# One table of a state-space backward pass is built in the stage that uses it instead of two stages earlier

## The chip, the cores and the metric

The kernel runs on one core of one Trainium2 chip. The metric is device time in microseconds, the median of several executions. One execution was also taken by the hardware profiler; its page and its trace are what the text reads. TensorE is PE in the profile (PEld is its load of weights), VectorE is DVE, ScalarE is ACT, GpSimd is POOL, SyncE is SP. SP, ACT and POOL issue DMAs.

## What is computed

The reference is a block with two branches over x (2048 rows of 512 columns), and the kernel returns its output and all gradients for an incoming gradient:

```python
xn = layernorm(x)
s  = ssm(xn)                  # y = causal convolution of xn with K along the 2048 rows, + xn * Dskip
g  = silu(silu(xn @ w1) @ w2) # w1: 512 x 1792, w2: 1792 x 512
out = x + s * g
# K[d, l] = Re sum_n C[d,n] * exp(dt[d] * A[d,n] * l) * dt[d] * B[d,n],  n = 0..127, A, B, C complex
```

The gradients of A, B and C need, for each channel d and state n, sums over l of dK[d, l] times the power exp(dt A l). The powers are the tables of this text. A position l is split into a coarse and a fine part, l = 128 h + 8 w (with some special positions), so that each power is a product of a coarse table X (41 entries a channel) and a fine table Y (16 entries a channel: exponents 0, 8, ..., 120). CY is Y multiplied by C and dt B; it is used for K itself.

## The kernel before

The kernel is six stages written one behind the other; inside each stage the order of instructions on every engine is the order in which the Python calls them (the scheduling is manual), and generators are advanced step by step to lay the work of several parts beside one another.

**Stage 1** (0 to about 180 us in the trace) runs the feed-forward branch and computes base powers of the tables for all channels (`power_phases`, L427), which go to DRAM as `XYd`: 28 entries, of which 0 to 16 are bases for X, 17 to 19 the low bases of Y (exponents 8, 16, 24), 20 to 23 its high bases (0, 32, 64, 96) and 24 to 27 the high bases of CY.

**Stage 2**, here called the table stage (about 180 to 300 us), goes through four blocks b of 128 channels. For each block, `open_tables` (L751) loads X's bases, `ld_tab` (L743) loads the eleven entries of Y and CY as XYc, `copy_tables` (L781) spreads them with ScalarE copies into tiles Y and CY (L786), and `chunk_tables` (L795) multiplies out X (`prod`, L816 to L823), CY and Y (`quads`, L802 to L813) on the DVE. A call of `quads` is six DVE instructions: one product of 3072 elements a partition (L806), two of 1536 (L810), and two sums of 1536 (L811, L813). `chunk_K` (L848) multiplies CY by X on TensorE (ps_k, L860), and ScalarE puts the result into Kout; after block 3, `store_K` (L872) writes K to DRAM as Kud and `load_K` (L885) brings it back in another layout as K_b. `gen_xt` (L921) transposes X on TensorE in eleven groups (L932), ScalarE evicts them (L934), and SP stores them to DRAM as XTd; `gen_yt` (L941) does the same with Y, in two calls of two groups a block (L950, L951), to YTd. XT and YT share four buffers of one tag. Beside these, the loop of `stage_2` runs forward transforms of xn and of DS on TensorE (ps_f, L998, evicted by L999), a radix step on the DVE (`radix`, L92 to L98), and transposes of w2 (L973 to L977).

The order in the loop over j (L1054 to L1076): Y's product of block b (`next(k.gt[b])`, L1062) is called at j = 0 of block b for b = 0 and 1, the one of block 2 at L1078, that of block 3 at L1093. X's bases of block b + 2 are loaded at j = 10 (L1074), on the SP queue behind the XTd stores of block b.

**Stage 3 and stage 4** (about 300 to 440 us) transform K_b (ps_f, L1164), multiply spectra on the DVE (`cplx_mul`, L101) and transform back. The last XT and YT groups of block 3 are evicted between these transforms.

**Stage 5** has two halves. The first ends at about 480 us. The second, here called the slab stage (480 to 575 us), lays three things beside one another on TensorE: `conv` (L1680; 16 matmuls of 512 columns, ps_v), the gradient of w2 (`Dw2.run`, L1589; two halves of 8 matmuls of 512 columns, ps_w), and the **slabs** (`Slabs`, L1717). A slab is a quarter of a block: 16 slabs, three steps each (`steps`, L1809):

- step A: `P2(i, 0)`, 16 matmuls of 256 columns (ps_V, L1769) evicted by ScalarE to Vb (L1771); then `Gb(i + 1)` on the DVE (two instructions, L1757).
- step B: `P2(i, 1)`, the same for the other half; then `load(i + 3)`, which issues the slab's XT (XTl, on SP and POOL) and its YT (YTl, on POOL, L1747).
- step C: `D3(i)` on the DVE (three instructions, L1780 and L1783), Vb times YT; then `P3(i - 1)`, eight matmuls of 512 columns (ps_S, L1798) of the slab before.

The loop over ft from 4 to 13 (L1693) places them: a conv while there is one (ft 4 to 9), one step, half a w2 product, two steps, the other half, two steps. PSUM has two buffers for ps_v and ps_V together (tag pd) and three for ps_w and the transposes (tag ps).

**Stage 6** (575 us to the end) is the backward pass of the feed-forward branch, led by `dh` (L1857).

The few lines that set the order of the slab stage:

```python
for ft in range(4, FT):
    t0 = 2 * (ft - 2)
    if t0 < T:
        conv(t0)
    some(1)
    for _ in w2.run(ft):
        some(2)
    some(2)
```

Of the kernel before, what the change touches and what calls it, by code (L numbers as in the profile page):

```python
# [14 lines left out]
P = 128  # L15
# [120 lines left out]
def kernel(ctx, tc, A_u, A_A_re, A_A_im, A_B_re, A_B_im, A_C_re, A_C_im, A_log_dt, A_Dskip, B_x, B_w1, B_w2, grad_out,  # L136
# [28 lines left out]
    k.XTd = dr.tile([NB, 64 * NR, 2, P], BF16, name="XTd"); k.YTd = dr.tile([16, P, 2, 4, P], BF16, name="YTd")  # L165
# [556 lines left out]
def tables_open(k, fs):  # L722

    lo = k.left
    k.mm = lo.open("mm")
    sa = lo.open("sa")
    k.tabs, k.gt, k.gc = {}, {}, {}
    k.slot = [(sa, sa), None]
    XY = fs.tile([P, 11, 2, 64, 2], BF16, name="XYc", tag="aT")

    def more():
        k.nc.gpsimd.dma_start(XY[:].rearrange("p i c q e -> p i (c q e)"), k.XYd[:, 17:NT, 0])
# [4 lines left out]
    k.gt[0] = chunk_tables(k, 0)  # L737
    k.nt0 = 0
    k.ko = lo.open("ko"); k.xc = lo.open("xc")
    k.Kout = k.ko.tile([P, NH, P], BF16, name="Kout")  # L740


def ld_tab(k, b):  # L743

    XY = k.xc.tile([P, 11, 2, 64, 2], BF16, name="XYc", tag="XYc")
    k.nc.sync.dma_start(XY[:].rearrange("p i c q e -> p i (c q e)"), k.XYd[:, 17:NT, b])
    k.gc[b] = copy_tables(k, b, XY)
    k.gt[b] = chunk_tables(k, b)
# [13 lines left out]
def open_y(k, b):  # L762

    slot, cys = k.slot[b % 2]
    k.tabs[b]["Y"] = slot.tile([P, 2, 64, 16, 2], BF16, name="Y", tag="Y")
    k.tabs[b]["CY"] = cys.tile([P, 2, 64, 16, 2], BF16, name="CY", tag="CY")
# [13 lines left out]

def copy_tables(k, b, XY):  # L781

    Y, CY = k.tabs[b]["Y"], k.tabs[b]["CY"]
# [11 lines left out]
def chunk_tables(k, b):  # L795
# [6 lines left out]
    def quads(x, op0, op1):  # L802
        fl = lambda m: m.rearrange("p c q (a b) e -> p (c q) a b e", a=4)
        m1, m2 = mt("m1", 12), mt("m2", 12)
        qd = x[:].rearrange("p c q (a b) e -> p c q a b e", a=4)
        TT(out=fl(m1), in0=qd.rearrange("p c q a b e -> p (c q) a b e")[:, :, :, 0:1].to_broadcast([P, 128, 4, 3, 2]),  # L806
           in1=cq(t["Y"], slice(1, 4)).unsqueeze(2).to_broadcast([P, 128, 4, 3, 2]), op=ALU.mult)
        q4 = lambda m, c: m[:, c].rearrange("p q (a b) e -> p q a b e", a=4)
        for c in range(2):
            TT(out=q4(m2, c), in0=qd[:, c, :, :, 0:1].to_broadcast([P, 64, 4, 3, 2]), in1=t["Y"][:, 1 - c, :, 1:4].unsqueeze(2).to_broadcast([P, 64, 4, 3, 2]), op=ALU.mult)  # L810
        TT(out=qd[:, 0, :, :, 1:4], in0=q4(m1, 0), in1=q4(m1, 1), op=op0)  # L811
        i, j = (0, 1) if op1 == ALU.add else (1, 0)
        TT(out=qd[:, 1, :, :, 1:4], in0=q4(m2, i), in1=q4(m2, j), op=op1)  # L813
# [18 lines left out]
    if b == 0:  # L832
        quads(t["CY"], ALU.add, ALU.subtract)
        yield
# [6 lines left out]
    if b:  # L841
        quads(t["CY"], ALU.add, ALU.subtract)
        yield
    quads(t["Y"], ALU.subtract, ALU.add)
    yield

# [74 lines left out]
def gen_xt(k, xs, b):  # L921

    nc = k.nc
    X = k.tabs[b]["X"][:].rearrange("p h c e q -> p h c (e q)")
    for n in range(11):
        ks = range(4 * n, min(4 * n + 4, 41))
        if n % 2 == 0:
            XT = xs.tile([P, 8, 2, P], BF16, name="XT", tag="XT", bufs=4)
        pt = k.ps.tile([P, 4, 2, P], BF16, name="pt_xt", tag="ps")
        for j, kk in enumerate(ks):  # L930
            for c in range(2):
                nc.tensor.transpose(out=pt[:, j, c], in_=X[:, kk, c], identity=k.ident[:])  # L932
# [5 lines left out]
        yield  # L938


def gen_yt(k, xs, i0):  # L941
    nc = k.nc
    YT = xs.tile([P, 2, 2, 4, P], BF16, name="YT", tag="XT", bufs=4)
    for i in (i0, i0 + 1):
        b, u, s, q0 = slab(i)
        Y = k.tabs[b]["Y"]
        pt = k.ps.tile([P, 2, 4, P], BF16, name="pt_yt", tag="ps")
        for c in range(2):
            for b4 in range(4):
                nc.tensor.transpose(out=pt[:, c, b4, :], in_=Y[:, c, q0 + 4 * b4:q0 + 4 * b4 + 4].rearrange("p w l e -> p (w l e)"), identity=k.ident[:])  # L950
        nc.scalar.copy(out=YT[:, i - i0], in_=pt[:])  # L951
        if i > i0:
            k.put(k.YTd[i0:i0 + 2].rearrange("i p c b n -> p i (c b n)"), YT[:].rearrange("p i c b n -> p i (c b n)"))
        yield
# [48 lines left out]
def stage_2(k):  # L1003
# [35 lines left out]
    for b in range(NB):  # L1039
# [3 lines left out]
        gy = [gen_yt(k, k.xs, i) for i in (4 * b, 4 * b + 2)]  # L1043
        sl = [gx] * 11 + [g for g in gy for _ in range(2)]
# [4 lines left out]
        if b == 2:  # L1049
            sl, gy2 = sl[:11], sl[11:]  # L1050
# [3 lines left out]
        for j in range(15):  # L1054
# [6 lines left out]
            if j == 0 and b < 2:  # L1061
                next(k.gt[b])  # L1062
# [15 lines left out]
    next(k.gt[2])  # L1078
    for g in gy2:
        next(g)  # L1080
# [12 lines left out]
    next(k.gt[3])  # L1093
    sl = iter(sl)
    for n in range(8):
        next(next(sl))
# [18 lines left out]
    return gk, sl, held  # L1115
# [151 lines left out]
def stage_3(k, gk, sl, held):  # L1267
# [3 lines left out]
    for n, _ in enumerate(gk, 1):  # L1271
# [4 lines left out]
        for g in (next(sl, None) for _ in range(n >= 4)):  # L1276
            if g is not None:
                next(g)
# [325 lines left out]
def stage_5(k):  # L1604
# [60 lines left out]
    S.load(0, nc.gpsimd)  # L1665
    for j in (1, 2):
        nc.gpsimd.memset(S.flat(j), 0.0)
# [49 lines left out]
class Slabs:  # L1717
# [3 lines left out]
    def __init__(self, k, sw):  # L1721
        self.k, self.sw = k, sw
        self.XT, self.YT, self.G, self.V, self.T, self.psS, self.S_sb = {}, {}, {}, {}, {}, {}, {}
# [14 lines left out]
    def load(self, i, q=None):  # L1738
        k, nc = self.k, self.k.nc
        dma = (q or nc.sync).dma_start  # L1740
        YT = self.YT[i] = self.sw.tile([P, 2, 4, P], BF16, name="YTl", tag="YT", bufs=4)
# [5 lines left out]
        nc.gpsimd.dma_start(YT[:], k.YTd[i])  # L1747
# [85 lines left out]
class Bwd:  # L1833
# [23 lines left out]
    def dh(self, n):  # L1857
# [5 lines left out]
        sd = self.fw.tile([P, 2, 512], BF16, name="sd", tag="sd")  # L1863
# [37 lines left out]
    def dx(self, tc_, dhT):  # L1901
# [3 lines left out]
        for t in range(4 * tc_, 4 * tc_ + 4):  # L1905
# [6 lines left out]
            m12 = fw.tile([P, 2], F32, name="m12", tag="m12"); c12 = fw.tile([P, 2], F32, name="c12", tag="c12")  # L1912
# [9 lines left out]
    def rest(self):  # L1922
# [8 lines left out]
        O1 = fw.tile([P, D], BF16, name="O1", tag="O1")  # L1931
# [7 lines left out]
def stage_6(k):  # L1939
# [5 lines left out]
    k.fx = ro.open("fx", 2)  # L1945
# [64 lines left out]
    ro.close("fp4", "ww", "fx", "fw", "wt", "tip", "tf2", "tfp")  # L2010
# [31 lines left out]
```

## Time and profile before

| | us |
|---|---|
| median of 3 executions | 753.71 |
| lowest, highest of them | 752.43, 753.82 |
| the profiled execution | 754.35 |
| its span (first to last instruction) | 752.2 |
| TensorE busy | 665.2 (88%) |
| DVE busy | 619.8 (82%) |
| ScalarE busy | 444.4 (59%) |
| POOL busy | 124.4 (17%) |

The span lies inside the profiled execution's time; 2.15 us of that execution are around it. Times inside the text count from the span's start. "Idle before, releaser" in the profile's rows says how long an engine stood before an instruction and what ended that. A row of a timeline gives the start, the time that it covers, the engine, the line, what is written and read, and how many instructions are merged in it. Instructions of one engine overlap a little at their ends, so that a sequence takes less than the sum of its rows.

### The profile page before, as it was taken

What the parts mean: (1) busy time and instruction counts of PE and PEld (TensorE: products, weight loads), DVE (VectorE), ACT (ScalarE), POOL (GpSimd) and SP (SyncE); (2) the same over time, 40 slices, a digit from 0 to 9 for tenths busy, and PEclk for the clock granted to TensorE, in tenths of its full rate; (3) what the DMA queues carried; (4) which work ended last, traced back from release to release, by engine and by line L of the source; (5) the groups of instructions that cost most, each with busy time, mean ns of one, the idle gap of its engine ahead of it and who ended that gap; (6) DMA issues with size and microseconds to landing.
All of it is one profiled execution on the core that took longest, in us unless ns stands there. A gap on an engine that the chain in (4) does not pass through costs nothing. (4 is left out here: it accounts for less than half of the span.)

```text
span 752.2 us, 13787 instructions
## 1 busy us (share of the span) xinstructions
PE 665.2 (88%) x5356; PEld 347.0 (46%) x5356; DVE 619.8 (82%) x965; ACT 444.4 (59%) x541; POOL 124.4 (17%) x192
## 2 busy tenths in 40 slices
PE   4768978798978777999999899989999999889998
PEld 2434444353646566454444344434444554444444
DVE  6899999998999798699999999654685579988810
ACT  4789888986769857375435322244566765764211
POOL 2334071021002003000012111311131000111210
PEclk9999998999989997999999999999999999999999
DMA  9647766899898969899667889798895987788591
GB/s 270 235 160 254 239 212 240 273 315 362 266 318 280 289 189 215 302 375 380 247 248 250 298 324 339 227 331 303 279 298 170 283 230 225 234 251 280 186 344 52
DMA packets 153155, 198.86 MB, mean 264 GB/s; under 512 B 29405, under 2 KB 114788, under 8 KB 147170
## 3 DMA queue, kind: packets, MB, share of 16 engines
q1 hardware_dynamic: 133314, 129.48, 54.6%
q0 software_dynamic: 11840, 54.07, 20.0%
q10 hardware_dynamic: 7936, 14.43, 5.9%
q8 instruction: 42, 0.69, 0.4%
q14 instruction: 23, 0.19, 0.1%
HBM read 112.72 MB, written 83.38 MB: 261 GB/s over the span
## 5 line engine op out<-in xcount | busy, mean ns | idle before, releaser
L607 PE MATMUL ps_h<-XNT,W 128*128 128x512 bf16 x224 | 61.1, 423 | 13.8 <-ACT hs L610 13.8
L1188 PEld LDWEIGHTS <-TIs 128*128 128x128 bf16 x384 | 37.3, 98 | 50.4 <-issue 4.4
L580 PE MATMUL ps_o<-W,aT 128*128 128x512 bf16 x224 | 54.3, 391 | 1.8 <-DVE ak L76 1.8
L1869 PE MATMUL ps_da<-DOT,W2T 128*128 128x512 bf16 x224 | 52.9, 379 | 1.5 <-ACT DOT L1849 1.1
L1908 PE MATMUL ps_dx<-W1T,dhT 128*128 128x512 bf16 x224 | 52.9, 379 | 0.0
L1870 DVE TENSOR_TENSOR dhT<-ps_da,sd 128x1024 bf16<-128x1024 f32 x28 | 34.1, 1221 | 22.0 <-ACT sd L132 16.3
L1594 PE MATMUL ps_w<-DO_all,AW 128*128 128x512 bf16 x224 | 52.0, 380 | 0.0
L1992 PE MATMUL ps_w<-dhc,xn 128*128 128x448 bf16 x256 | 49.3, 352 | 1.0 <-DMA dhc<-dhd 1.0
L1780 DVE TENSOR_TENSOR T<-Vb,YTl 128x2048 bf16<-128x2048 bf16 x16 | 19.6, 1223 | 35.9 <-ACT Vb L1771 35.6
L1164 PEld LDWEIGHTS <-TFs 128*128 128x128 bf16 x312 | 30.2, 98 | 37.4 <-issue 2.8
L934 ACT COPY XT<-pt_xt 128x1024 bf16<-128x1024 bf16 (+1 forms) x44 | 41.3, 1004 | 4.0 <-DMA XTd<-XT 3.0
L1771 ACT CAST Vb<-ps_V 128x1024 bf16<-128x1024 f32 x32 | 31.7, 1013 | 17.9 <-PE ps_V L1769 12.0
L607 PEld LDWEIGHTS <-W 128*128 128x128 bf16 x224 | 22.7, 105 | 39.4 <-issue 22.8
L1164 PE MATMUL ps_f<-K_b,TFs 128*128 128x512 bf16 x168 | 38.9, 379 | 1.7 <-DMA K_b<-Kud 1.2
L1917 ACT ACTIVATE dxn<-dxn,c,rstd 128x512 f32<-128x512 f32 x16 | 13.0, 814 | 45.0 <-DVE c L1916 45.0
L580 PEld LDWEIGHTS <-aT 128*128 128x128 bf16 x224 | 22.8, 102 | 31.2 <-issue 7.4
L1992 PEld LDWEIGHTS <-xn 128*128 128x128 bf16 x256 | 25.0, 98 | 24.9 <-DMA dhc<-dhd 1.5
L998 PE MATMUL ps_f<-xn,TFs 128*128 128x512 bf16 x128 | 33.1, 414 | 2.4 <-DMA TFs<-TFd 2.4
L1893 ACT COPY dhk<-pt_dh 128x1024 bf16<-128x1024 bf16 x28 | 28.0, 1001 | 10.2 <-PE pt_dh L1891 10.2
L1869 PEld LDWEIGHTS <-W2T 128*128 128x128 bf16 x224 | 21.6, 98 | 26.8 <-issue 2.2
L1164 PE MATMUL ps_f<-DS,TFs 128*128 128x512 bf16 x144 | 33.0, 379 | 0.7 <-ACT S_s L1442 0.7
L1594 PEld LDWEIGHTS <-AW 128*128 128x128 bf16 x224 | 20.2, 98 | 26.7 <-issue 4.7
(345 smaller groups left out, 1570.6 us busy)
## 6 DMA issues: line engine op xcount, KB each, us to landing
TIs<-TId SPq DMA_DIRECT2D x24, 512.0 KB, 6.5
XTd<-XT SPq DMA_DIRECT2D x20, 512.0 KB, 4.5
XTl<-XTd SPq DMA_DIRECT2D x15, 512.0 KB, 8.1
hTd<-hs SPq DMA_DIRECT2D x28, 256.0 KB, 3.5
akd<-ak SPq DMA_DIRECT2D x28, 256.0 KB, 3.6
UXl<-UXd POOLq DMA_DIRECT2D x7, 1024.0 KB, 7.9
dhd<-dhk SPq DMA_DIRECT2D x28, 256.0 KB, 5.3
XYd<-XYg SPq DMA_DIRECT2D x25, 256.0 KB, 4.5
```

The source lines that it names most:

```text
L580: nc.tensor.matmul(out=pso[:], lhsT=aT[:, ft, tt * P:(tt + 1) * P], rhs=W2[:, ft, :], start=(ft == 0), stop=(ft == FT - 1))
L607: nc.tensor.matmul(out=ps[:, j], lhsT=W1[:, dk, ft * P:(ft + 1) * P], rhs=XNT[:, dk], start=(dk == 0), stop=(dk == DK - 1))
L934: nc.scalar.copy(out=XT[:, j0:j0 + len(ks)], in_=pt[:, 0:len(ks)])
L998: nc.tensor.matmul(out=ps[:, c, :], lhsT=TFs[:, t1 + 4 * j, c, :], rhs=src[:, t1 + 4 * j, :], start=(j == 0), stop=(j == 3))
L1164: nc.tensor.matmul(out=ps[:, c, :], lhsT=tab(j), rhs=at(t1 + 4 * j), start=(n == 0), stop=(n == 4 * len(terms) - 1))
L1188: nc.tensor.matmul(out=ps[:, j, :], lhsT=TIs[:, j, 2 * kt + c, :], rhs=B[kt][:, c, (t0 + j) % 4, :], start=(kt == 0 and c == 0), stop=(kt ...
L1594: nc.tensor.matmul(out=ps[:], lhsT=A[:, t, :], rhs=k.DO[:, t, :], start=(t == 0), stop=(t == T - 1))
L1771: nc.scalar.copy(out=self.V[i][:, g2], in_=ps[:].rearrange("p b c n -> p c b n"))
L1869: nc.tensor.matmul(out=ps[:, j], lhsT=self.W2T[:, ft // 2, dk, j * P:(j + 1) * P], rhs=self.DOT[tc_][:, dk], start=(dk == 0), stop=(dk == ...
L1870: nc.vector.tensor_tensor(out=self.dhT[:, f0:f0 + 2, :], in0=ps[:], in1=sd[:], op=ALU.mult)
L1908: nc.tensor.matmul(out=psx[:], lhsT=dhT[:, ft, t % 4 * P:(t % 4 + 1) * P], rhs=self.W1T[:, ft, :], start=(ft == 0), stop=(ft == FT - 1))
L1992: nc.tensor.matmul(out=ps[:], lhsT=k.xn[:, t, dk * P:(dk + 1) * P], rhs=ch[i][:, t, :], start=(t == 0), stop=(t == T - 1))
```

## The change

Y is no longer built, transposed or stored in the table stage. The tile Y, `gen_yt`, the DRAM tensor YTd and the loads YTl go. What is left of Y in the table stage is its three low bases (tile Yb), which CY's product needs; XYc has seven entries instead of eleven. XT has six buffers instead of four, and all eleven groups of block 3 are transposed in the table stage.

In the slab stage, `load_y` loads the seven bases of a block from XYd on POOL (XYl and XYo); `Yq(i)` spreads a slab's high bases with two ScalarE copies of 128 elements a partition (and, once a block, the low bases with one of 768) and multiplies the slab's Y out on the DVE in six instructions of 384 elements; `Yt(i)` transposes it on TensorE in eight 128x128 blocks, and ScalarE evicts them to YT. `Yq(i + 1)` is called in step B of slab i, `Yt(i + 1)` in step C behind `P3(i - 1)`. In stage 6, sd, m12, c12 and O1 move to a pool of their own, opened when the slabs' memory is given back.

```diff
 def copy_tables(k, b, XY):
-    def cp(x, o, i, n):
-        k.nc.scalar.copy(out=cq(x, o), in_=XY[:, i:i + n].rearrange("p i c q e -> p (c q) i e"))
-    cp(Y, slice(1, 4), 0, 3)
     yield
-    cp(Y, slice(0, 16, 4), 3, 4)
+    low_copy(k, k.tabs[b]["Yb"], XY[:, 0:3])
     yield
-    cp(CY, slice(0, 16, 4), 7, 4)
+    k.nc.scalar.copy(out=cq(k.tabs[b]["CY"], slice(0, 16, 4)), in_=XY[:, 3:7].rearrange("p i c q e -> p (c q) i e"))
     yield
...
+def cplx_quads(k, x, low, m1, m2, op0, op1):
...
+    else:
+        for c in range(2):
+            TT(out=q4(m1, c), in0=ba(c), in1=lw(c), op=ALU.mult)
+    for c in range(2):
+        TT(out=q4(m2, c), in0=ba(c), in1=lw(1 - c), op=ALU.mult)
+    TT(out=qd[:, 0, :, :, 1:4], in0=q4(m1, 0), in1=q4(m1, 1), op=op0)
+    i, j = (0, 1) if op1 == ALU.add else (1, 0)
+    TT(out=qd[:, 1, :, :, 1:4], in0=q4(m2, i), in1=q4(m2, j), op=op1)
...
 def chunk_tables(k, b, XY):
...
-    quads(t["Y"], ALU.subtract, ALU.add)
-    yield
...
 def gen_xt(k, xs, b):
...
-            XT = xs.tile([P, 8, 2, P], BF16, name="XT", tag="XT", bufs=4)
+            XT = xs.tile([P, 8, 2, P], BF16, name="XT", tag="XT", bufs=6)
...
-def gen_yt(k, xs, i0):
...
 class Slabs:
     def load(self, i, q=None):
...
-        nc.gpsimd.dma_start(YT[:], k.YTd[i])
+
+    def load_y(self, b):
+        k = self.k
+        ld = {}
+        for nm, o, n, bufs in (("XYl", 20, 4, 2), ("XYo", 17, 3, 1)):
+            t = ld[nm] = self.sw.tile([P, n, 2, 64, 2], BF16, name=nm, tag=nm, bufs=bufs)
+            k.nc.gpsimd.dma_start(t[:].rearrange("p i c q e -> p i (c q e)"), k.XYd[:, o:o + n, b])
+        self.XY[b] = ld["XYl"], ld["XYo"]
+
+    def Yq(self, i):
+
+        k, nc = self.k, self.k.nc
+        b, u, s, q0 = slab(i)
+        XY, low = self.XY[b]
+        if i % 4 == 0:
+            Yb = self.Yb = self.sw.tile([P, 2, 64, 3, 2], BF16, name="Yb", tag="Yb")
+            low_copy(k, Yb, low[:])
+        Y = self.Y[i] = self.sw.tile([P, 2, 16, 16, 2], BF16, name="Ys", tag="Ys", bufs=1)
+        for c in range(2):
+            nc.scalar.copy(out=Y[:, c, :, 0:16:4], in_=XY[:, :, c, q0:q0 + 16].rearrange("p a q e -> p q a e"))
+        m1, m2 = (self.sw.tile([P, 2, 16, 12, 2], BF16, name=f"Ym{j}", tag=f"Ym{j}") for j in range(2))
+        cplx_quads(k, Y[:], self.Yb[:, :, q0:q0 + 16], m1[:], m2[:], ALU.subtract, ALU.add)
+
+    def Yt(self, i):
+        k, nc = self.k, self.k.nc
+        Y = self.Y.pop(i)
+        pt = k.ps.tile([P, 2, 4, P], BF16, name="pt_yt", tag="ps")
+        for c in range(2):
+            for b4 in range(4):
+                nc.tensor.transpose(out=pt[:, c, b4, :], in_=Y[:, c, 4 * b4:4 * b4 + 4].rearrange("p w l e -> p (w l e)"), identity=k.ident[:])
+        YT = self.YT[i] = self.sw.tile([P, 2, 4, P], BF16, name="YT", tag="YT", bufs=2)
+        nc.scalar.copy(out=YT[:], in_=pt[:])
...
             self.P2(i, 0)
             if i + 1 < 16:
                 self.Gb(i + 1)
+            if i == 0:
+                self.Yq(0)
             yield
             self.P2(i, 1)
             self.XT.pop(i), self.G.pop(i)
             if i + 3 < 16:
                 self.load(i + 3)
+            if i % 4 == 1 and i < 12:
+                self.load_y(i // 4 + 1)
+            if i == 0:
+                self.Yt(0)
+            if i + 1 < 16:
+                self.Yq(i + 1)
             yield
             self.D3(i)
             if i:
                 self.P3(i - 1)
+            if i + 1 < 16:
+                self.Yt(i + 1)
...
-        sd = self.fw.tile([P, 2, 512], BF16, name="sd", tag="sd")
+        sd = k.fw2.tile([P, 2, 512], BF16, name="sd", tag="sd")
```

More of the change, by code (lines that the diff above doesn't have):

```diff
@@ L164 @@
     k.Snd = dr.tile([2, 2, D, N], F32, name="Snd")
-    k.XTd = dr.tile([NB, 64 * NR, 2, P], BF16, name="XTd"); k.YTd = dr.tile([16, P, 2, 4, P], BF16, name="YTd")
+    k.XTd = dr.tile([NB, 64 * NR, 2, P], BF16, name="XTd")
     k.dhd = dr.tile([P, T, F], BF16, name="dhd")
@@ L740, in tables_open, with ld_xy @@
     k.Kout = k.ko.tile([P, NH, P], BF16, name="Kout")
+def ld_xy(k, XY, b, q):
+    for o, i, n in ((0, 17, 3), (3, 24, 4)):
+        q.dma_start(XY[:, o:o + n].rearrange("p i c q e -> p i (c q e)"), k.XYd[:, i:i + n, b])
 def ld_tab(k, b):
-    XY = k.xc.tile([P, 11, 2, 64, 2], BF16, name="XYc", tag="XYc")
-    k.nc.sync.dma_start(XY[:].rearrange("p i c q e -> p i (c q e)"), k.XYd[:, 17:NT, b])
+    XY = k.xc.tile([P, 7, 2, 64, 2], BF16, name="XYc", tag="XYc")
+    ld_xy(k, XY, b, k.nc.sync)
     k.gc[b] = copy_tables(k, b, XY)
-    k.gt[b] = chunk_tables(k, b)
+    k.gt[b] = chunk_tables(k, b, XY)
 def open_tables(k, b, q, fn=None):
@@ L801, in chunk_tables, with quads @@
     mt = lambda nm, n: k.mm.tile([P, 4096], BF16, name=nm, tag="cm_t" + nm[1])[:, 0:256 * n].rearrange("p (c q n e) -> p c q n e", c=2, q=64, e=2)
[L802 to L813, printed above, removed]
+    def quads():
+        cplx_quads(k, t["CY"][:], t["Yb"][:], mt("m1", 12), mt("m2", 12), ALU.add, ALU.subtract)
     Xf = X[:].rearrange("p h c e q -> p h c (e q)")
@@ L937, in gen_xt @@
             k.put(k.XTd[b, P * k0:P * k1].rearrange("(k p) c n -> p k c n", p=P), XT[:, 0:k1 - k0])
-        yield
-def gen_yt(k, xs, i0):
[L942 to L953, printed above, removed]
         yield
@@ L1042, in stage_2 @@
         gx = gen_xt(k, k.xs, b)
-        gy = [gen_yt(k, k.xs, i) for i in (4 * b, 4 * b + 2)]
-        sl = [gx] * 11 + [g for g in gy for _ in range(2)]
+        sl = [gx] * 11
         if b == 3:
@@ L1092, in stage_2 @@
     radix(3)
[L1093 to L1096, printed above, removed]
+    for g in sl:
+        next(g)
     XD = st["D"]["A"]
@@ L1114, in stage_2 @@
     k.dskb = dskip_out(k)
-    return gk, sl, held
+    return gk, held
 def rad_inv(k, pool, tag, PX):
@@ L1264, in gen_kt, with stage_3 @@
         yield
-def stage_3(k, gk, sl, held):
+def stage_3(k, gk, held):
     nc = k.nc
```

52 lines of the change are left out of this document (26 added, 26 removed).

## Prediction

> **What bounds the kernel now.** I read the page's busy shares first, then the busy time by stretches, then the DVE's and TensorE's rows in order of time, and last the waits of single lines. A difference of 0.2% (1.5 us) is about what a measurement of this kernel can tell from no change.
>
> Busy time by stretches (us; busy time and count of each engine, granted clock, DMA share, GB/s):
>
> ```profile
> 240.00:260.00 20.00, 15.91 (x338) 12.38 (x334) 15.87 (x28) 18.47 (x22) 1.82 (x3) 0.91 0.98 298
> 380.00:420.00 40.00, 39.30 (x184) 17.73 (x182) 39.22 (x38) 15.95 (x18) 7.18 (x14) 1.00 0.82 285
> 500.00:520.00 20.00, 17.94 (x180) 8.04 (x179) 9.60 (x14) 8.53 (x10) 3.17 (x6) 1.00 0.96 337
> 540.00:560.00 20.00, 19.33 (x237) 8.84 (x234) 15.78 (x22) 12.52 (x15) 5.83 (x11) 1.00 0.87 290
> ```
>
> There are three regimes. In the table stage (first row) ScalarE, DVE and the DMA engines are all near full and hand the limit to one another. From 314 to 480 us the DVE has no gap to speak of, so whatever the table stage gains arrives whole at 480. In the slab stage (last two rows; 480.6 to 575.7) TensorE is the bound, its instructions stand in a fixed order, and the DVE is half idle at first and four fifths busy later. The change takes work out of the first regime and puts it into the third, and the order of instructions says that it does: no Y is multiplied or transposed before the slab stage.
>
> **Table stage: what goes.** The rows of the DVE in order of time:
>
> ```profile
> 250.69 1.22 DVE L98 TENSOR_TENSOR XU<-r_t 128x2048 bf16<-128x2048 bf16 x1
> 255.97 1.09 DVE L819 TENSOR_TENSOR m<-X 128x1792 bf16<-128x1792 bf16 x1 [4.06 <-DMA X<-XYd]
> ...
> 271.57 0.95 DVE L813 TENSOR_TENSOR CY<-m 128x1536 bf16<-128x1536 bf16 x1
> 272.44 1.75 DVE L806 TENSOR_TENSOR m<-Y 128x3072 bf16<-128x3072 bf16 x1
> ```
>
> Y's products are six instructions a block, 1.75 + 2x0.95 + 0.96 + 0.95 = 5.5 us, in queue 5.3. Four blocks give 22 us of DVE time, but only blocks 0 and 1 (193.5 and 225.2 us) stand ahead of block 3's CY, which ends at 272.4 and starts the way to the kernel's K: TensorE's ps_k, Kout, Kud, K_b, and at 302.4 the transform that keeps the DVE full from 314. Blocks 2 and 3 come after it. So 10.6 us are on the path, not 22. With these gone the DVE waits earlier for X: it already waits 4.06 us for block 3's X (above), which is loaded on SP behind the last XTd store, which follows ScalarE's 44 XT evictions. ScalarE has one gap (1.85 us) between 223.6 and 249.3. Ahead of that it loses block 0's four YT evictions (0.92 each in queue), the strided copy of Y (1.22) and, because XT gets six buffers of its own and no slot that YT held, the 5.2 us that it waited for an XTd store from 216.6 to 221.8: 10 us. SP's queue and the DMA engines give some of that back, so I take block 3's X 8 us earlier (its issue at 242.5 against 250.9); CY moves by 8, not 10.6. Two YTd stores of 512 KB stand on SP and in the DMA engines (share 0.97) just ahead of K_b's loads, which take 14 us to land; without them I take 2 us more. TensorE must be ready then: without pt_yt (279.3 to 284.2) it does two classes, eleven XT groups instead of eight at ScalarE's 0.92 each, and ps_dsk, and comes out at 291 to 292, about where K_b lands. Sum **-10 us**; bounds -5 (SP and the DMA engines keep X where it was but for the shorter queue) and -14 (10.6 and the whole of the DMA time of the two stores, 1 MB at 290 GB/s). The smaller XYc load is inside this; ScalarE's remaining low copy (0.88) was there before. Stage 3 loses four YT groups (0.45 us of TensorE and 1.02 of ScalarE each) that lie beside a full DVE: nothing.
>
> **Slab stage: what comes.** For slab i+1, in program order: step B of slab i issues P2(i,1) with its Vb eviction, then Yq(i+1) (two ScalarE copies of 128 elements, six DVE products of 384); step C issues D3(i) on the DVE, then P3(i-1) and the eight transposes of Yt(i+1) on TensorE. The copies are queued on ScalarE behind the Vb that waits for P2(i,1), the products behind the copies, the transposes behind P3(i-1), with all of TensorE's later work behind the transposes. A slab ahead is thus a third of a slab ahead. Prices by form:
>
> ```profile
> L806 DVE TENSOR_TENSOR m<-Y 128x3072 bf16<-128x3072 bf16 x4 | 7.0, 1750 | 0.0
> L95 DVE TENSOR_TENSOR r_t<-XU 128x512 bf16<-128x512 bf16 x5 | 2.1, 418 | 0.0
> L819 DVE TENSOR_TENSOR m<-X 128x256 bf16<-128x256 bf16 x4 | 1.1, 282 | 0.0
> ```
>
> 384 elements lie between the last two: 0.35 us each, and in a queue these rows start 0.07 to 0.08 earlier than their lengths say, so 0.27; six are 1.63 us. A 128-element copy is not in the trace: ScalarE's 128x256 XT piece takes 0.41 to 0.48, a 128x4 activation 0.20; I take 0.3, in queue 0.2, bounds 0.15 and 0.4.
>
> Now the order of time on TensorE, with what waits where:
>
> ```profile
> 491.15 0.62 PE L1769 MATMUL ps_V<-XTl,Gbd 128*32 128x256 bf16 x16
> 491.70 1.90 PE L1594 MATMUL ps_w<-DO_all,AW 128*128 128x512 bf16 x8
> ...
> 506.68 0.62 PE L1769 MATMUL ps_V<-XTl,Gbd 128*32 128x256 bf16 x16 [2.06 <-DMA XTl<-XTd]
> 507.24 3.63 PE L1188 MATMUL ps_v<-BG,TIs 128*128 128x512 bf16 x16
> ```
>
> P2(0,1) starts at 491.15 and its Vb at 491.82 (+0.67); Vb holds ScalarE 0.92; the two copies and the hand-over 0.5; the products with theirs 1.73. Yt(i+1) can start 3.8 us after P2(i,1). TensorE gets there after P2 (0.5), what stands between steps B and C, and P3 (0.72): it waits 2.6 us less what stands between. The loop puts five steps beside each ft; following the 48 steps, nothing stands between for seven slabs (i = 0, 4, 5, 9, 10, 11, 14), half a w2 product (1.83) for six, a conv (3.55) for two. So 7 x 2.6 + 6 x 0.8 + 2 x 0 = 23 us. On top: slab 0, whose own Y is made in step A behind Vb(0,0), low copy and all, 2.1; the low copies of blocks 1 to 3 (0.77 in queue) on the same way, 2.3; and where ScalarE still has the eviction of ps_w (0.5) or of the last YT ahead of Vb, some eight times 0.5, 4. Stalls 31 us. The transposes themselves: eight start 0.45 us in all (as eight pt_xt do between 316.03 and 316.48), sixteen times, 7. Against it: TensorE now comes later to loads that it waits for (2.06 above, 0.84 and 0.49 at 560 and 565), -3. POOL loses sixteen YTl loads (0.55 us each) and gets eight XYl and XYo loads, behind the first XTl and ahead of later ones: nothing waits for them but the first, issued at 482 and needed at 490.7, when an XTl load issued then takes 7.8. Sum **+36 us** (31+7-3, and 1 for copies nearer 0.25). Bounds: products at 0.24 and copies at 0.15 give +28; unoverlapped products of 0.42 (the 512 row) and copies of 0.4 give +57. The DVE does 3.55 us a slab now and 5.2 then; where no conv is left (from 547) it is gapless at 3.55 already, but TensorE's stalled slab takes longer than 5.2, so this adds nothing more.
>
> **Clock.** Stalls may cost clock. After 2.4 us idle the granted clock was 0.63 (188 to 192) and 31 matmuls took 8.46 us instead of 6.9 at a conv's rate (16 in 3.55); in the slab stage the 2.06 us wait above was followed by a conv at full speed and 1.00. I take +2, bounds 0 and 11 x 1.6 = 18 (the seven stalls with nothing between, slab 0's, and those behind low copies are near or over 2 us). The Trainium skill (TensorE: Matmul & The Clock Gate, on the HAM clock gate) says that the clock falls after an idle window of about 3.4 us; by it only two stalls would count (slab 1's, behind YT(0)'s eviction, 3.4; slab 12's, behind a low copy, 3.8), +3. The drop after 2.4 us is shorter than that window, so the trace speaks for the dearer end.
>
> **Stage 6.** sd moves to memory that S_sb and YT leave; its second buffer overlaps S_sb, whose store to Snd is issued at 576.35 and lands in 2.8 to 7.6 us; sd x2 ran from 577.4 to 579.4, and dhT after it has 1.1 us to spare. **+1**, bounds 0 and 4.
>
> **Sum.** The profiled execution: span 752.2, with 2.15 around it 754.35. 752.2 - 10 + 36 + 2 + 1 = 781.2, with 2.15 around it 783.4; that execution was 0.64 over the median of 753.71, so **783** for a median.
>
> **Rivals.** (1) Forecast, 783; its own range 770 to 797; chance 0.70. (2) The clock falls at each long stall: 783 - 2 + 18 = 799; for it the table stage's slices of 0.50 to 0.75, against it the slab stage's 1.00; 0.15. (3) The products come in time, as "a slab ahead" says, and only the transposes and the DVE's bound count: the last seven slabs at 5.2 instead of 4.65 give 4; 754.35 - 10 + 7 + 4 + 1 = 756; it needs the chain of 3.8 us under 1.2, and Vb alone is over that; 0.08. (4) Faster: the table stage yields its 22 us whole, because K's path starts earlier than CY of block 3 suggests and ScalarE's 20 us go too, while the slab stage pays as in (3): 754.35 - 22 + 7 + 4 + 1 = 744. It decides where the slab stage costs under 22; for it is the DVE without a gap from 188 to 251.9; against it the wait for X at 252 and the two blocks behind CY; 0.05. (5) Stalls and gains cancel within 0.2%, an edge of (3); 0.02.
>
> Faster by over 0.2%: 0.05; within: 0.02; slower: 0.93. The range takes (1)'s bounds and half of (2): 768 to 801.
>
> **What would show it.** In the changed profile the transposes of Ys should have, as the releaser of their idle time, the DVE's Ys product, 25 to 40 us in all; the slab stage should last 125 to 140 us instead of 95; the last product of CY should end near 264 and TensorE's transform of K begin near 292. If the idle time before the transposes is under 10 us, the order of queues does not bind as I say; if the transform still begins at 300, the table stage's gain is wrong; a granted clock under 0.9 in the slab stage makes (2) right.

## The result, and the profile after

| | before | after |
|---|---|---|
| median of six executions (us) | 754.0 (752.4 to 757.1) | 784.4 (780.3 to 788.5) |
| profiled execution, its span (us) | 754.35, 752.2 | 780.43, 778.7 |
| first matmul of the slab stage's first conv (us) | 477.6 | 467.0 |
| from there to stage 6's first matmul (us) | 97.8 | 135.5 |
| from there to the end (us) | 176.8 | 176.2 |

The change makes the kernel slower: ratio 1.039, 95% interval 1.034 to 1.044. The forecast was 783. The table stage gains 10.6 us, the slab stage loses 37.7 (its first conv to stage 6; the forecast counted it from 480.6, as 95 us), the rest is unchanged within 0.6.

Busy time by stretches of the changed kernel (columns as before: PE, PEld, DVE, ScalarE, POOL with counts; clock; DMA share; GB/s):

```profile
240.00:260.00 20.00, 15.17 (x361) 11.91 (x362) 19.40 (x35) 17.19 (x21) 1.61 (x3) 0.91 0.92 278
380.00:420.00 40.00, 36.29 (x154) 15.90 (x158) 38.23 (x47) 17.93 (x19) 7.40 (x17) 0.93 0.72 255
500.00:520.00 20.00, 14.61 (x170) 6.94 (x162) 12.37 (x29) 12.24 (x19) 1.57 (x3) 1.00 0.58 190
540.00:560.00 20.00, 16.28 (x181) 7.58 (x181) 11.97 (x25) 12.95 (x20) 1.51 (x3) 1.00 0.41 126
```

First row: the DVE is now full there (19.40 of 20, before 15.87), because the work of block 3 has moved up. Second row: the DVE remains the bound of stages 3 and 4 (38.23 of 40, before 39.22). Last two rows: TensorE, which set the pace at 17.94 and 19.33 of 20 before, falls to 14.61 and 16.28. The DVE is not full either (12.37, 11.97), nor are ScalarE and the DMA engines. Where no engine is full, the engines wait for each other in turn; the rows below show how.

The table stage, DVE in order of time (releaser in brackets):

```profile
225.41 1.09 DVE L834 TENSOR_TENSOR m<-X 128x1792 bf16<-128x1792 bf16 x1 [5.30 <-DMA X<-XYd]
...
247.43 1.09 DVE L834 TENSOR_TENSOR m<-X 128x1792 bf16<-128x1792 bf16 x1 [0.54 <-DMA X<-XYd]
...
263.01 0.96 DVE L817 TENSOR_TENSOR CY<-m 128x1536 bf16<-128x1536 bf16 x1
```

CY of block 3 ends at 263.97 (before 272.5). The DVE still waits for a table's bases, but one block earlier: 5.30 us for block 2's X, 0.54 for block 3's (before 4.06). TensorE then comes out of its classes and XT groups just as K_b is there:

```profile
279.23 0.61 PE L945 MATMUL pt_xt<-ident_bfloat,X 128*128 128x128 bf16 x8 [4.23 <-ACT XT L947]
...
289.32 4.48 PE L1151 MATMUL ps_f<-K_b,TFs 128*128 128x512 bf16 x19
```

The transform of K runs without a gap from 289.32; before, it ran from 302.44 behind a wait for K_b. The DVE does not follow it at once: it first waits for a store, and comes to the transform's output at 302.98 (before 314.07), although ScalarE had evicted what it needs by 300.9:

```profile
299.10 1.23 DVE L97 TENSOR_TENSOR BK<-r_t 128x2048 bf16<-128x2048 bf16 x1 [9.93 <-DMA UXd<-XU]
```

The slab stage by forms:

```profile
L1760 PE MATMUL pt_yt<-ident_bfloat,Ys 128*128 128x128 bf16 x128 | 11.1, 229 | 27.6 <-DVE Ys L815 27.6
L812 DVE TENSOR_TENSOR Ym<-Ys,Yb 128x384 bf16<-128x384 bf16 x32 | 10.0, 355 | 44.7 <-ACT Ys L1750 44.7
L1750 ACT COPY Ys<-XYl 128x128 bf16<-128x128 bf16 x32 | 8.3, 317 | 0.0
```

Read the idle columns as a chain: TensorE stood 27.6 us before its transposes for the DVE's sum (L815), the DVE 44.7 us before its products for ScalarE's copies. One link of it, on TensorE, ScalarE and the DVE:

```profile
526.12 0.62 PE L1784 MATMUL ps_V<-XTl,Gbd 128*32 128x256 bf16 x16
...
529.62 1.01 PE L1760 MATMUL pt_yt<-ident_bfloat,Ys 128*128 128x128 bf16 x8 [2.45 <-DVE Ys L815]
530.85 2.62 PE L1578 MATMUL ps_w<-DO_all,AW 128*128 128x512 bf16 x7 [0.22 <-issue]
```

```profile
526.79 1.01 ACT L1786 CAST Vb<-ps_V 128x1024 bf16<-128x1024 f32 x1 [1.02 <-PE ps_V L1784]
527.70 0.51 ACT L1750 COPY Ys<-XYl 128x128 bf16<-128x128 bf16 x2
```

```profile
528.04 0.63 DVE L812 TENSOR_TENSOR Ym<-Ys,Yb 128x384 bf16<-128x384 bf16 x2 [4.68 <-ACT Ys L1750]
528.58 0.62 DVE L814 TENSOR_TENSOR Ym<-Ys,Yb 128x384 bf16<-128x384 bf16 x2
529.12 0.35 DVE L815 TENSOR_TENSOR Ys<-Ym 128x384 bf16<-128x384 bf16 x1
```

P2 at 526.12, Vb at 526.79, copies at 527.70, products and sums from 528.04, transposes at 529.62: 3.5 us from P2, of which TensorE has its P2 and P3 (1.05) to do and stands for 2.45. The DVE had been idle for 4.68 us when the copies came: it was not the slow one.

### The profile page after: what moved, and what is told of

The parts are those of the page before. It is cut to its first block, busy times and chain, and to the rows that moved or that the text cites. A ratio compares the mean times of both kernels' runs of the same rounds, so it can differ in the third digit from the quotient of the medians.

```text
span 778.7 us, 13820 instructions
## 1 busy us (share of the span) xinstructions
PE 660.2 (85%) x5285; PEld 345.4 (44%) x5356; DVE 625.0 (80%) x1041; ACT 450.3 (58%) x573; POOL 124.4 (16%) x185
## 4 chain that ended last, share of the span: by engine, by line
PE 38%; DVE 22%; ACT 12%; issue 7%; DMA 6%; SPq 1%; ACTq 0%; DVEq 0%; POOL 0%; POOLq 0%
PE ps_f L1151 11%; PE ps_v L1175 5%; PE ps_w L2017 5%; PE ps_dx L1933 3%; PE ps_w L1578 3%; PE ps_da L1894 3%; ACT Vb L1786 2%; DMA dhc<-dhd 2%; DMA X<-XYd 2%; DVE cm_t L106 1%; PE ps_V L1784 1%; DVE cm_t L107 1%; PE pt_yt L1760 1%; PE ps_k L873 1%; DVE dhT L1895 1%
## 5 line engine op out<-in xcount | busy, mean ns | idle before, releaser
L607 PE MATMUL ps_h<-XNT,W 128*128 128x512 bf16 x212 | 57.8, 414 | 14.4 <-ACT hs L610 13.6
L812 DVE TENSOR_TENSOR Ym<-Ys,Yb 128x384 bf16<-128x384 bf16 x32 | 10.0, 355 | 44.7 <-ACT Ys L1750 44.7
L1151 PE MATMUL ps_f<-DS,TFs 128*128 128x512 bf16 x142 | 35.1, 397 | 5.1 <-ACT S_s L1426 4.1
L1760 PE MATMUL pt_yt<-ident_bfloat,Ys 128*128 128x128 bf16 x128 | 11.1, 229 | 27.6 <-DVE Ys L815 27.6
```

The source lines that it names most:

```text
L607: nc.tensor.matmul(out=ps[:, j], lhsT=W1[:, dk, ft * P:(ft + 1) * P], rhs=XNT[:, dk], start=(dk == 0), stop=(dk == DK - 1))
L1151: nc.tensor.matmul(out=ps[:, c, :], lhsT=tab(j), rhs=at(t1 + 4 * j), start=(n == 0), stop=(n == 4 * len(terms) - 1))
```

## The experiments

The theory (T1): Y of slab i+1 is begun only in step B of slab i, behind P2 and Vb, and the in-order TensorE reaches its transposes before the chain of copies and products is through. Rivals: T2, the added instructions cost the time by themselves (26 us of DVE, 7 of TensorE); T3, it is the clock. In the table, "conv" and "stage" are the two times of the result's table in that kernel's profile, "idle" is TensorE's before the transposes of the slab stage; ratios are to the kernel before on the same chip, where its median was 754.0 to 757.2.

| run | median (us) | ratio, 95% interval | conv | stage | idle |
|---|---|---|---|---|---|
| before | | | 477.6 | 97.8 | |
| after | 784.4 | 1.039 (1.034 to 1.044) | 467.0 | 135.5 | 27.6 |
| e1_lead | 761.5 | 1.010 (1.007 to 1.013) | 466.4 | 113.7 | 7.3 |
| e2_late_t | 764.3 | 1.013 (1.011 to 1.015) | 468.0 | 116.9 | 12.4 |
| e3_no_yq | 752.6 | 0.997 (0.995 to 0.999) | 470.0 | 104.3 | 1.6 |
| e4_no_yt | 753.9 | 0.997 (0.995 to 1.000) | 470.2 | 105.8 | |
| e5_table_only | 744.2 | 0.985 (0.980 to 0.989) | 467.8 | 97.7 | |
| e6_slab_only | 793.6 | 1.049 (1.044 to 1.054) | 478.3 | 134.3 | 27.6 |
| e7_lead_early | 757.7 | 1.002 (0.9995 to 1.005) | 470.1 | 108.5 | 4.4 |
| e8_lead_pool | 770.8 | 1.019 (1.015 to 1.023) | 467.8 | 124.6 | 11.8 |
| e9_half | 754.6 | 0.996 (0.993 to 0.9999) | 470.8 | 104.7 | 2.7 |
| e10_half_held | 761.1 | 1.004 (1.001 to 1.007) | 477.5 | 104.6 | 2.8 |
| e11_before_vb | 770.8 | 1.016 (1.013 to 1.019) | 468.9 | 123.3 | 15.6 |
| e12_half_tuned | 748.9 | 0.992 (0.989 to 0.995) | 470.2 | 98.9 | 0.2 |

The table stage of the change is in nine of these kernels unaltered (after, e1 to e5, e7, e8, e11), and conv begins in their single profiled executions between 466.4 and 470.2: the gain read from one profile is known to some 4 us.

**e1_lead: the same work, begun a slab earlier.**

```diff
@@ steps, step B
-            if i % 4 == 1 and i < 12:
+            if i % 4 == 0 and i < 12:
                 self.load_y(i // 4 + 1)
...
-            if i + 1 < 16:
-                self.Yq(i + 1)
+            if i == 0:
+                self.Yq(1)
@@ step C
                 self.Yt(i + 1)
+            if i + 2 < 16:
+                self.Yq(i + 2)
```

> The same work as the changed kernel; only the place in the order differs: the copies and products of slab i+2 are issued in step C of slab i, right behind the transposes of slab i+1 (slab 1's own in step B of slab 0), and load_y one slab earlier. T1 (TensorE waits for a chain that starts too late: Vb, copies, products): the transposes find their Ys ready except for slab 1, their idle time falls from 27.6 to under 6 us, the slab stage from 133 to 106-112 us (transposes 7, the DVE's bound of the last slabs 4), the time to 752-762. T2 (the added instructions themselves cost it: 26 us of DVE and 7 of TensorE): nothing is taken away, 776-788. T3 (clock lost to something other than these waits): slab stage still above 120 us and clock at most 0.965.

The idle time before the transposes fell to 7.3 us and the stage by 21.8; 761.5, at the slow end of T1's range. Idle time and stage are a little over what I expected (under 6, and 106 to 112). T2 as the whole cost is refuted, since not an instruction was taken away, and T3 with it (it put the stage above 120). The row of the transposes, then two stretches:

```profile
L1760 PE MATMUL pt_yt<-ident_bfloat,Ys 128*128 128x128 bf16 x128 | 10.4, 225 | 7.3 <-DVE Ys L815 6.5 <-ACT Vb L1786 0.7
```

```profile
480.00:490.00 10.00, 5.55 (x42) 2.68 (x40) 7.23 (x21) 4.87 (x10) 2.06 (x3) 0.73 0.95 315
...
540.00:560.00 20.00, 18.22 (x242) 9.27 (x235) 18.00 (x38) 15.99 (x25) 4.23 (x8) 1.00 0.79 257
```

What is left lies at two places: the start (slabs 0 and 1, TensorE busy 5.55 of 10 at a clock of 0.73), which this run does not mend, and the end, where the DVE is now as full as TensorE.

**e2_late_t: the products where they were, the transposes a step later** (`Yt(i)` behind `P2(i, 0)` in step A in place of `Yt(i + 1)` in step C).

> The same work again; here the products stay where the change put them (slab i+1's in step B of slab i) and the transposes of slab i+1 move from step C of slab i to step A of slab i+1, behind its first P2. T1: TensorE comes 0.5 us (the P2) and one more gap between steps later; with a gap of 1.83 or more in most slabs until the conv's are gone, the 3.8 us chain is nearly covered: idle ahead of the transposes 4-10 us, time 756-768, some of it a new wait of D3 for the YT eviction, which now ends later. T2: 776-788. T3: as in the run before.

12.4 us idle, 764.3: moving the other end of the chain helps nearly as much, as T1 says. The idle time is over what I expected; part of it has a new releaser, ScalarE's Vb. I take this to be the PSUM buffer of the transposes, whose last user's eviction now stands behind Vb; that was not tried by itself:

```profile
L1760 PE MATMUL pt_yt<-ident_bfloat,Ys 128*128 128x128 bf16 x128 | 10.3, 218 | 12.4 <-DVE Ys L815 8.3 <-ACT Vb L1786 3.9
```

**e11_before_vb: what the chain is made of** (`Yq(i + 1)` at the head of step B, ahead of `P2(i, 1)`, in place of behind it).

> The changed kernel with Yq(i+1) issued at the head of step B, ahead of P2(i,1) and its Vb, and all else in place (slab 1's behind it as before). T1 with the chain as the prediction made it up (P2 0.67, Vb 0.92, copies 0.5, products 1.73): what is left of the chain is 2.2 us from the head of step B, so a slab with nothing in between waits 1.0 in place of 2.6 and one with half a w2 product not at all: idle ahead of the transposes 27.6 to 10-15, time 764-772. Rival (the products wait for the DVE's own queue, not for Vb): idle over 20, time over 775.

```profile
L1760 PE MATMUL pt_yt<-ident_bfloat,Ys 128*128 128x128 bf16 x128 | 11.1, 229 | 15.6 <-DVE Ys L815 13.0 <-ACT S_sb L1816 1.5 <-ACT AW L1582 0.9
```

15.6 us and 770.8: the 12 us that went are what P2 and Vb ahead of the copies cost. The rival (DVE's own queue) is refuted; that 15.6 is a little over the 10 to 15 that I gave it is ScalarE's evictions of S_sb and ps_w (2.4), which now stand between.

**e3_no_yq and e4_no_yt: one half of the added work at a time.** e3 drops `Yq` for slabs 1 to 15 and transposes slab 0's Ys again; e4 drops `Yt` for them and lets D3 read slab 0's YT.

> Leaves out the copies and products of slabs 1 to 15; their transposes turn slab 0's Ys again, so the output is not the reference's Y for them. TensorE's added work is all there, the wait is not. T1: slab stage 133 - 27.6 - 2 to 3 of clock = 102-104 us, time 749-754, the transposes' idle time under 3 us. T2 with the DVE's instructions as the cost: the same 749-754, so this run tells T1 from T2 only together with the next. T2 with TensorE's transposes as the cost: still over 770. T3: over 765.

> Leaves out the transposes and evictions of slabs 1 to 15 (D3 reads slab 0's YT for all, so the output is not the reference's), and keeps all copies and products at their places in the queues. T1: the products end as late as before, but nobody on TensorE waits for them: slab stage 95-102 us (the DVE's 5.2 us a slab against TensorE's 4.65 in the last seven gives up to 4), time 744-752. T2 (the DVE's 26 us are the cost): the slab stage stays at 120 us or more, time over 765. T3: over 765.

The stretch from 540 to 560 us, e3 and then e4:

```profile
540.00:560.00 20.00, 20.00 (x282) 10.77 (x280) 17.16 (x24) 15.93 (x19) 5.28 (x9) 1.00 0.84 285
```

```profile
540.00:560.00 20.00, 17.60 (x229) 8.34 (x227) 20.00 (x45) 13.00 (x22) 5.58 (x10) 1.00 0.83 273
```

With the transposes alone TensorE is full (20.00 of 20) and the stage lasts 6.5 us longer than before. With the copies and products alone the DVE is full and TensorE is not: 8.0 us longer, twice the 4 that I expected, and 753.9 in place of 744 to 752. Together 14.5; the changed kernel's stage is 37.7 longer. So some 23 us are neither half's own cost but the wait of one for the other. e1's stage, 15.9 over before, is close to the sum of the two halves.

**e5_table_only and e6_slab_only: do the two stages add up?** e5 keeps the table stage of the change and drops `Yq` and `Yt` of slabs 1 to 15; e6 keeps the table stage of the kernel before, YTd and all, and has the slab stage of the change.

> The table stage of the change alone: slab 0's Y is made and transposed, and its YT serves all sixteen slabs (copies, products, transposes of slabs 1 to 15 are left out, so the output is not the reference's). If the two stages add up: conv resumes about 10 us earlier than in the kernel before and the slab stage lasts 95-98 us: 742-747. If the slab stage gives part of it back (loads that TensorE now waits for, since it comes 10 us earlier): 747-752, with waits for XTl of 3 us and more. If the whole 22 us of DVE work counted: 734 or less.

> The slab stage of the change alone: the table stage of the kernel before, which still builds, transposes and stores Y (nobody reads it), and the slab stage of the changed kernel. If the two stages add up: conv resumes near 479.6, the slab stage lasts 131-135 us, idle ahead of the transposes 25-30 us: 788-796. If the waits come from TensorE's arriving 10 us earlier at loads or at a late DVE: idle under 20 us, below 785.

They do: e5 gains 11 us at 744.2 with a stage of 97.7 us (before 97.8), e6 loses 39 at 793.6 with a stage of 134.3 and, to a tenth, the changed kernel's idle time:

```profile
L1802 PE MATMUL pt_yt<-ident_bfloat,Ys 128*128 128x128 bf16 x128 | 11.1, 229 | 27.6 <-DVE Ys L816 27.6
```

So the waits do not come from TensorE's arriving earlier. The gain of 22 us (the forecast's fourth rival) is refuted.

**e7_lead_early: slab 0's Y early too.** e1 with `S.Yq(0)` behind the second conv and `Yt(0)`, `Yq(1)` ahead of slab 0's first P2.

> The run with the products a whole slab ahead (e1), and slab 0's copies and products issued behind the second conv, its transposes and slab 1's products ahead of slab 0's first P2. T1: the waits of slabs 0 and 1 (1.59 and 2.87 in e1), and the slow matmuls behind them (clock 0.73 in that stretch) go: 5 to 8 us off e1's 761.5, 753-757, idle ahead of the transposes under 3 us. What is left over the kernel before's slab stage is then the transposes (6, as e3 measured) and the full DVE (8 to 9, as e4 measured), against 10 of the table stage: within 3 us of the kernel before. Rival (the added work as such costs what e1 still shows): no change, 759-763.

757.7, 4 us faster than e1 (5 to 8 expected) and indistinguishable from the kernel before (1.002, 0.9995 to 1.005). The stage is 108.5; from 540 to 560 us the DVE is busy for 19.52 of 20 and TensorE for 17.85. All sixteen Y's in this stage leave the DVE full at its end, and the change at its best is about even.

**e8_lead_pool: half of the products on POOL.** e7 with two of each slab's four products (those into m2) and their sum on `nc.gpsimd`.

> As the run before, with half of each slab's Y (two products and their sum) on POOL in place of the DVE, which leaves the DVE three instructions, 0.9 us a slab. If the full DVE is what holds the last slabs: 3 to 6 us faster than e7, 748-753. If POOL's instructions (nearest row: 1.43 us for 512 float32 elements, so an estimated 1.1 for 384) come too late for the transposes or hold up the DVE: transposes wait for POOL, or the DVE's products last longer than their 0.35 and T12's than their 1.22 and 0.68: 756 or more.

13 us slower than e7. By forms:

```profile
L815 POOL TENSOR_TENSOR Ym<-Ys,Yb 128x384 bf16<-128x384 bf16 x32 | 36.8, 1168 | 30.6 <-ACT Ys L1752 30.5
L1800 DVE TENSOR_TENSOR T<-Vb,YT 128x1024 bf16<-128x1024 bf16 x32 | 29.5, 962 | 0.0
L813 DVE TENSOR_TENSOR Ym<-Ys,Yb 128x384 bf16<-128x384 bf16 x32 | 24.6, 808 | 10.8 <-ACT Ys L1752 10.7
L1797 DVE TENSOR_TENSOR T<-Vb,YT 128x2048 bf16<-128x2048 bf16 x16 | 19.5, 1217 | 3.7 <-ACT Vb L1788 3.5
```

POOL's product is 1.17 us, near the estimate of 1.1. But the DVE's product beside it is 0.81 in place of 0.35, and D3's 1024-element products (T<-Vb,YT) 0.96 in place of 0.68; D3's 2048-element one, which in the rows below lies beside none of POOL's products, keeps its 1.22. The DVE and POOL in order of time show the collision:

```profile
545.22 1.29 DVE L1800 TENSOR_TENSOR T<-Vb,YT 128x1024 bf16<-128x1024 bf16 x2
546.42 2.00 DVE L813 TENSOR_TENSOR Ym<-Ys,Yb 128x384 bf16<-128x384 bf16 x2
...
551.67 2.66 DVE L1800 TENSOR_TENSOR T<-Vb,YT 128x1024 bf16<-128x1024 bf16 x2
```

```profile
546.07 2.14 POOL L815 TENSOR_TENSOR Ym<-Ys,Yb 128x384 bf16<-128x384 bf16 x2
...
551.51 2.28 POOL L815 TENSOR_TENSOR Ym<-Ys,Yb 128x384 bf16<-128x384 bf16 x2 [1.79 <-ACT Ys L1752]
```

Two of D3's products take 1.29 us at 545.22, where POOL's next product does not start until 546.07, and 2.66 at 551.67, beside two of POOL's. The DVE lost more than it was relieved of: its three instructions left take 2.2 us a slab (two of 0.81 and a sum of 0.60) where the six took 2.1, and D3's products 0.56 more. TensorE's wait before the transposes is 11.8 us, 4.4 in e7. The Trainium skill (SBUF — State Buffer, on SBUF's two separate sides) says that the two engines share a pair of ports under an exclusive lock, held for a whole instruction; the rows above agree with that.

**e9_half and e10_half_held: only the blocks whose Y is on the path.** By the forecast's reading, Y of blocks 0 and 1 stands ahead of block 3's CY, that of blocks 2 and 3 behind it, where the DVE is not late. e9 therefore takes the kernel before, drops Y of blocks 0 and 1 from its table stage, and makes those eight slabs' Y as e7 does; slabs 8 to 15 keep YTd and YTl.

```diff
-    quads(t["Y"], ALU.subtract, ALU.add)
-    yield
+    if b > 1:
+        quads(t["Y"], ALU.subtract, ALU.add)
+        yield
...
-        sl = [gx] * 11 + [g for g in gy for _ in range(2)]
+        sl = [gx] * 11 + [g for g in gy for _ in range(2)] * (b > 1)
...
-            if j == 0 and b < 2:
-                next(k.gt[b])
@@ steps, step A
+            if i > 6 and i + 1 < 16:
+                self.load_t(i + 1)   # YTl, two buffers
```

> Y of blocks 0 and 1 alone goes to the slab stage (slabs 0 to 7, products a whole slab ahead, slab 0's early, as in e7); Y of blocks 2 and 3 stays in the table stage as in the kernel before, is stored to YTd and loaded for slabs 8 to 15. If only blocks 0 and 1 stand on the path to K: CY of block 3 ends at 264 to 265 as in the changed kernel, conv resumes 7 to 9 us earlier than before (the 1 or 2 us of block 2's stores ahead of K_b's loads are not gained); the slab stage costs eight slabs' transposes, 3 to 4 us, 1 or 2 for the products beside a DVE that is not full there: 748-752, under the kernel before. Rival (all four blocks' Y make up the gain): CY as early, but conv resumes at 475 or later: 754 and more. Rival (slab stage's cost does not go with the number of slabs): slab stage 104 us and more, 755 and more.

CY of block 3 ends at 266.0, conv begins at 470.8, 6.8 us earlier (7 to 9 expected): most of the table stage's gain comes from two of the four blocks. The stage was not the 100 us that I expected but 104.7, as the rival had it (a cost that does not go with the number of slabs), and the kernel only just faster (0.996). The trace shows waits that come from neither the transposes nor the products. TensorE waited 2.7 us before slab 0's transposes, because ScalarE's low copy waited 2.43 us for XYo, and D3 4.1 us for YTl, whose load waited for the D3 two slabs before:

```profile
L1842 DVE TENSOR_TENSOR T<-Vb,YTl 128x2048 bf16<-128x2048 bf16 x8 | 9.8, 1223 | 9.6 <-ACT Vb L1833 5.5 <-DMA YTl<-YTd 4.1
```

e10 puts block 2's YTd stores on SP behind K_b's loads.

> As the run before, with block 2's two YTd stores issued on SP behind K_b's loads instead of ahead of them. If these stores are what delays K_b: the transform of K begins 1 to 3 us earlier than in e9, 746-750. If K_b lands when it does for another reason (TensorE's work ahead of the transform, which here still has block 2's transposes): no difference to e9.

Neither: 6.5 us slower than e9. K_b's first load on SP is issued at 279.30, in e9, behind the stores, at 279.09; but Kud's stores, which these loads need, are themselves issued 1.1 us later here (273.93 against 272.83). Counted from them, K_b's first load comes after 5.4 us in e10 and 6.3 in e9, and POOL's first load of K_b has another releaser, e9 first:

```profile
279.66 0.57 POOL L925 DMA_DIRECT2D K_b<-Kud  x1 [6.86 <-DMA YTd<-YT]
```

```profile
279.88 0.57 POOL L925 DMA_DIRECT2D K_b<-Kud  x1 [5.97 <-DMA Kud<-Kout]
```

So the stores held K_b's loads up by about 0.9 us. What cost more lies behind: ScalarE's evictions of XT begin 5.4 us later than in e9 (288.35 against 282.93), behind a K_b load by the trace, and then wait twice for YTd stores, which now keep XT's buffers; TensorE's transform of K follows (300.9 against 292.5). Why the first of these waits is 6.80 us was not settled.

```profile
288.35 3.76 ACT L962 COPY XT<-pt_xt 128x1024 bf16<-128x1024 bf16 x4 [6.80 <-DMA K_b<-Kud]
294.24 1.93 ACT L962 COPY XT<-pt_xt 128x1024 bf16<-128x1024 bf16 x2 [2.12 <-DMA YTd<-YT]
```

**e12_half_tuned: e9 without its leftover waits** (three changes at once; the YTl of the loads gets the third buffer as shown, and so does YT).

```diff
-    S.load(0, nc.gpsimd)
     S.load_y(0)
+    S.load(0, nc.gpsimd)
...
-        m1, m2 = (self.sw.tile([P, 2, 16, 12, 2], BF16, name=f"Ym{j}", tag=f"Ym{j}") for j in range(2))
+        Ym = k.mm.tile([P, 2, 2, 16, 12, 2], BF16, name="Ym", tag=f"cm_t{1 + (i + 1) % 2}")
+        m1, m2 = Ym[:, 0], Ym[:, 1]
...
-        YT = self.YT[i] = self.sw.tile([P, 2, 4, P], BF16, name="YTl", tag="YT", bufs=2)
+        YT = self.YT[i] = self.sw.tile([P, 2, 4, P], BF16, name="YTl", tag="YT", bufs=3)
```

> As e9, with its three leftover waits taken away: block 0's bases are loaded ahead of slab 0's XTl, so that ScalarE's low copy need not wait for them (2.4 us in e9, which made TensorE wait 2.7 ahead of the first transposes and ran the next half w2 product at 2.9 in place of 1.9); YT has three buffers, so that a YTl load need not wait for the D3 two slabs before (4.1 us of DVE waits in e9); the products' temporaries lie in the T12 buffer that the next D3 takes, which pays for the memory. If these waits are what e9's slab stage has over its transposes: slab stage 103.4 to 98-100 us, 748-752, faster than the kernel before by 0.5 to 1%. Rival (e9's slab stage is long because the DVE is fuller in slabs 0 to 7): no change to e9, ratio 0.996.

748.9: faster than the kernel before by 0.8% (0.5 to 1.1). The stage is 98.9 us, where the rival had e9's unchanged. D3's wait for YTl is down from 4.1 to 1.7 us, and TensorE is full again:

```profile
480.00:490.00 10.00, 9.04 (x107) 4.64 (x106) 9.28 (x25) 8.00 (x12) 2.59 (x4) 1.00 1.01 322
...
540.00:560.00 20.00, 19.31 (x262) 9.41 (x260) 17.13 (x25) 12.27 (x15) 8.07 (x16) 1.00 0.92 318
```

## Why the prediction was right, step by step

**Slab stage: the order of queues.** The forecast's main step held: a slab ahead was a third of a slab ahead. Its formula, a chain of 3.8 us less what stands between steps B and C, gave 2.6 us for seven slabs, 0.8 for six, nothing for two. Measured, in the order of the trace: the seven waited 2.86, 2.45, 2.45, 2.45, 2.45, 3.67 and 2.45, the six 0.98, 1.59, 1.72, 0.85, 0.98 and 1.13, the two nothing, slab 0 1.59 (2.1 forecast). The 3.67, 1.59 and 1.72 are the slabs behind low copies. What was too large in the 31 us is the term for ScalarE's other evictions ahead of Vb: 4 forecast; only the 2.86 shows one, about 0.4. The stalls came to 27.6.

**Prices.** The products took 0.35 us, as interpolated, the copies 0.32 (0.3 taken). Eight transposes were priced at 0.45 us from start to start, 7 in all; they took 0.45 to 0.66, and about 1.2 at two slabs where the clock had fallen, some 10 in all. With these the slab stage adds up to 27.6 + 10 - 3.4 and 3 of clock, 37, and 37.7 were measured. The forecast's 36 and 2 came near because stalls some 3 us too long met transposes 3 us too short: that part is luck. Y's `quads` in the table stage is five DVE instructions a block, not six as the text before says twice; the times used there, 5.5 us in all, are of the five. In the slab stage it is six.

**Table stage**, -10 forecast: 10.6 at the conv, and e5 alone gives 11 in time. The gain can be followed along the chain, in us earlier than before: CY of block 3 8.5 (8 forecast), Kud's stores 9.5, K_b's first load 11.1, the unbroken transform of K 13.1, the DVE's first instruction on its output 11.1, the conv 10.6. Between Kud's stores and K_b's loads lie 7.2 us before, 5.6 in the changed kernel: 1.6 of the 2 us that the forecast gave to the two YTd stores, which e9 and e10 bear out with 0.9. In the changed kernel the DVE waited, by the trace, for the store to UXd ahead of its BK and not for the transform, so that 11 of the 13 us arrived there. And what reached the DVE arrived whole, as forecast: from there to the conv it is busy for 160.4 of 164.1 us, before 160.7 of 163.6. One reading was off without changing the sum: block 3's X is loaded behind the XT evictions of blocks 0 and 1, 22 of the 44.

**Clock**, +2: the w2 matmuls of the slab stage took 399 ns on average, 380 before, 3 us in all; slow ones stand behind two of the seven waits over 2.4 us (clock 0.83 from 480 to 500, 0.91 from 520 to 540). The dearer rival, 799, needed eleven. The +2 was picked between bounds of 0 and 18 without a rule for which waits count, so that its coming near is luck. **Stage 6**, +1: nothing. The second sd waited 0.80 us for the store to Snd, as foreseen, but the first group takes 4.37 us in both traces.

**XTl**, -3: the waits of 3.4 us for these loads in the slab stage are gone.

**What the forecast did not price.** It said that the DVE's fuller queue "adds nothing more" beside the stalls, and 4 where there are none. In the changed kernel that is so, but e4 puts it at 8: the stalls hid a second bound that appears as soon as they go. Rival (3), 756, is near what e7 comes to (757.7), once its condition, products in time, is made true.

The sum for the profiled execution was 783.4, and it took 780.4; the median lies at 784.4. Executions of one kernel spread by several microseconds, the longer ones with a lower mean clock (780.3 at 0.965, 788.5 at 0.954), which the forecast did not treat, so that a median within 1.4 us of 783 is in part luck.

## What to carry to other kernels

"A step ahead" in the program is worth what stands between the two places in the queue of the engine that must not wait, so count it there, in microseconds, slab by slab, and begin the chain earlier by at least its own length before judging what the work costs. Move off the path only the part that is on it: beginning the chain earlier turned a loss of 3.9% into about nothing (e7), and building only the two blocks that gave most of the gain, with the leftover waits taken out, made it a gain of 0.8% (e12). When a stall goes, the engine that was filled behind it is the next bound.

## What the runs showed of the hardware

- **Clock after short waits.** In the changed kernel TensorE's clock fell behind one of the five waits of 2.45 us (transposes 1.01 in place of 0.65 us, seven matmuls of the next half w2 product 2.62) and behind the one of 2.86 (3.19), which follows slab 0's wait of 1.59 with only eight transposes between, but not behind the one of 3.67, after which a half w2 product took its usual 1.89. So the length of a single wait does not decide it. The Trainium skill (TensorE: Matmul & The Clock Gate, on the HAM clock gate) puts the fall after an idle window of about 3.4 us that runs free of the kernel. By it a wait of 3.67 may or may not hold a whole window, and one of 2.45 or 2.86 cannot; so the two falls here do not agree with it, if each wait is taken alone.
- **POOL beside the DVE.** A POOL product of 384 elements (1.17 us) stretched DVE products beside it from 0.35 to 0.81 us on average and two of 0.68 to 2.66 together. In this stage, where the DVE was full, moving the work to POOL cost 13 us.
